# Merged row sums, a shorter last key tile and smaller weight pieces in an attention kernel that feeds a mixture of experts

## The chip, the cores and the metric

The kernel runs on one core of one Trainium2 chip. The metric is the device time of one launch in microseconds (us). A program on one core has no second core to compare with, so a run is called slow here when it is more than 1.5% above the fastest run of the same kernel in the same job, and fast otherwise.

## The reference, cut to what matters

```python
# attention: 4 batches, 8 heads, 768 positions, head size 64, fp32
keep  = is_global(first 8 keys) | is_local(0 <= i - j < 96)
scores = q @ k.T / 8 + bias(head, distance);  scores[~keep] = -1e9
a = exp(scores - max);  a = a / (sum(a) + 1e-9);  x = a @ v
# experts: 3072 tokens, 512 wide, 8 experts of 384 tokens each
logits = x @ w_gate                       # balanced greedy assignment of tokens to experts
out[mask] = relu(x[mask] @ w1[e]) @ w2[e]
```

The kernel works in three stages: attention over 16 head pairs (two heads of one batch at a time), routing (six rounds of a search on the vector engine), and the eight experts.

## The kernel before

Per head pair the tensor engine (PE) computes scores, the scalar engine (ACT) takes the exponential, the vector engine (DVE) multiplies a bias-and-mask table, and PE multiplies by v. Another engine, Pool, issues the weight loads. Then one function forms the row sums of the exponentials and the gate logits in the same two tiles `pr` in PSUM. Row halves (`rg`) and query quarters (`gq`) give eight combinations of 64 operand rows and 32 output rows; the page lists their matmuls as `64*32`, and the prediction calls a combination a tile. In the records of the phase at 118.82 us the first matmuls of the eight start 6 or 7 ns apart, while two of 151 columns in the same combination start 128 or 129 ns apart. `t` is the head of the pair. Cuts are marked with `# ...`.

```python
def scores(n, g):
    ps = ps_s.tile([128, 2, 512], FP32, tag="ps")
    for i, q0, o, w in PIECES[g]:            # three key tiles of 159 columns, and 24 of the last
        for c in range(2):                   # upper and lower half of the key tile
            qa = q0 + (56 * c if i < NT - 1 else 0)
            for t in range(2):
                # ... r: the 64 rows of head t
                nc.tensor.matmul(ps[64*c : 64*c + 64, t, o : o + w], lhsT=kA[r, i, 64*c : 64*c + 64],
                                 rhs=qTt[r, qa : qa + w], start=True, stop=True, ...)

def sums(n):
    pr = [ps_t.tile([128, 192], FP32, tag="pt", ...) for rg in range(2)]
    # for every (gq, rg): a list of (columns, onesx[.., t, :], Ps[n, g][.., t, columns]) over pieces and heads t
    # ... the lists are issued in turn, one matmul of each (gq, rg) after the other
    for gq in (0, 1, 2, 3):
        for rg in range(2):                  # gate logits of head rg
            nc.tensor.matmul(pr[rg][32*gq : 32*gq + 32, :], lhsT=wgx[64*rg : 64*rg + 64, j, :],
                             rhs=oTs[n][64*rg : 64*rg + 64, :, gq, :], start=False, stop=True, ...)

def sums_out(n, pr):                         # sums and logits to the token layout
    for rg in range(2):
        nc.vector.transpose(out=LT[:, rg], in_=pr[rg])
    nc.vector.tensor_tensor(out=rs[n], in0=LT[:, 0, :, 16:18], in1=LT[:, 1, :, 16:18], op=ALU.add)
    nc.vector.reciprocal(rs[n], rs[n])
    # ... gate logits times rs; x scaled by rs in tok_out; every fourth pair a reduction into L_sb

# the loop over head pairs, every engine in the order written:
for n in range(NP + 2):
    # scores and exp of pair n, first half; v product of pair n-1; x transposes of pair n-2;
    # k and q transposes of pair n+1; second halves
    weight_piece()                           # one 512 KB load of expert weights on the Pool queue
    # ... mask(n, 1); sums(n-1); sums_out(n-1, pr)
while wpieces:
    weight_piece()                           # the rest of them
```

The softmax here doesn't subtract the row's maximum and nothing guards it: scores larger than these inputs give would overflow.

## Time and profile before

| | kernel before |
|---|---|
| time, median of the first 3 runs | 366.54 us (361.71 to 382.19) |
| profiled run (375.11 us): span | 373.3 us |
| its attention, to the last matmul of the sums | 201.8 us |
| from there to the first expert matmul | 72.0 us |
| from there to the end | 99.5 us |
| records of PE up to the end of attention (8116 matmuls and weight loads, 79 others, nearly all semaphore instructions) | 8195 |
| 16,384-byte packets of PE's instruction queue | 39 |
| stops at borders of 256 instructions, summed | 38.5 us |
| half-clock time of PE inside attention | 29.7 us |

The last two are worked out from the records of the trace: all records of PE are put in order of start and numbered from 0; the stop at a border is the time from record k-1 to record k for k = 449 + 256j. The half-clock time sums the windows in which the granted clock was 0.5. The profiled run is a launch of its own and 3.7% slower than the fastest of the runs: by the rule above it is slow. The prediction below shows the lines of the page and of the waits.

### The profile page before, as it was taken

To read this page: it belongs to the slowest core of one execution; us is meant where nothing else is said; L and a number is where in the kernel's file an instruction comes from. 1 tells how busy PE (TensorE), PEld (TensorE's weight loads), DVE (VectorE), ACT (ScalarE), POOL (GpSimd) and SP (SyncE) were. 2 spreads that over 40 slices of the span, in tenths; PEclk is the share of its full clock that TensorE was granted. 3 is DMA by queue.
4 is the path that set the end of the run, shared out by engine and by line. 5 is a ranking of instruction groups with operands and counts; after the bars stand their busy time and mean duration, and the time that the engine had idled before them with its cause. 6 is when DMAs were issued, how large, how long until landed. Compare 5 with 4: busy or idle time off the path is not lost. (4 is left out here: it accounts for less than half of the span.)

```text
span 373.3 us, 10787 instructions
## 1 busy us (share of the span) xinstructions
PE 270.2 (72%) x4684; PEld 201.5 (54%) x4684; DVE 168.5 (45%) x421; ACT 104.4 (28%) x192; POOL 114.9 (31%) x170
## 2 busy tenths in 40 slices
PE   3678889885979679789777232222479999999990
PEld 2676778775958569677656111111245555555540
DVE  4154546641746436466353766678313322223310
ACT  1665324341524314343110000000023244432230
POOL 8342123330333303323603000000477545433221
PEclk9999999996989979899896555555569999999996
DMA  8997986985597983847999993000134323322111
GB/s 164 236 252 155 188 175 136 241 193 100 125 191 153 199 174 98 149 90 149 183 211 209 226 214 62 0 0 1 42 101 129 98 84 115 112 84 86 56 60 63
DMA packets 58376, 49.49 MB, mean 133 GB/s; under 512 B 32977, under 2 KB 51921, under 8 KB 58321
## 3 DMA queue, kind: packets, MB, share of 16 engines
q0 software_dynamic: 15808, 26.22, 34.6%
q1 hardware_dynamic: 42512, 22.50, 24.5%
q8 instruction: 39, 0.64, 0.7%
q14 instruction: 17, 0.13, 0.1%
HBM read 56.05 MB, written 9.44 MB: 175 GB/s over the span
## 5 line engine op out<-in xcount | busy, mean ns | idle before, releaser
L292 PE MATMUL ps<-qT,kA 64*64 64x159 f32 (+1 forms) x1024 | 43.7, 293 | 23.3 <-issue 18.6
L327 PE MATMUL po<-P,v 64*64 64x151 f32 (+8 forms) x1088 | 49.5, 283 | 14.0 <-issue 13.2
L292 PEld LDWEIGHTS ps<-qT,kA 64*64 64x64 f32 x1024 | 36.7, 141 | 34.7 <-issue 28.9
L300 ACT ACTIVATE P<-ps 128x1002 f32<-128x1002 f32 x32 | 32.3, 1008 | 75.9 <-PE ps L292 75.9
L327 PEld LDWEIGHTS po<-P,v 64*64 64x64 f32 x1088 | 43.0, 145 | 17.1 <-issue 16.0
L271 POOL COPY kA<-kA 128x56 f32<-128x56 f32 x16 | 16.5, 1030 | 116.2 <-DVE kA L267 99.4
L801 ACT ACTIVATE hT<-ph 128x384 bf16<-128x384 f32 x64 | 31.4, 490 | 71.7 <-PE ph L798 71.1
L781 POOL DMA_INDIRECT xe<-x_tok,idi x24 | 23.0, 959 | 80.1 <-DVE idi L638 62.9
L798 PE MATMUL ph<-xT,w_all 128*128 128x384 bf16 x256 | 44.9, 336 | 0.1
L306 DVE TENSOR_TENSOR P<-P,Wm 128x1002 f32<-128x1002 f32 x32 | 40.3, 1261 | 2.4 <-ACT P L300 2.4
L396 DVE TENSOR_TENSOR x<-pk,rs 128x384 bf16<-128x384 f32 x32 | 17.6, 557 | 44.7 <-PE pk L389 43.6
L798 PEld LDWEIGHTS <-w_all 128*128 128x128 bf16 x256 | 25.7, 100 | 18.8 <-issue 2.5
L811 POOL DMA_INDIRECT out_dram<-ot,idi x24 | 23.5, 981 | 35.9 <-DVE ot L810 32.7
L355 PE MATMUL pr<-P,onesx 64*32 64x24 f32 (+18 forms) x1408 | 32.8, 263 | 0.0
L355 PEld LDWEIGHTS pr<-P,onesx 64*32 64x32 f32 x1408 | 29.5, 116 | 2.2
L810 DVE COPY ot<-po 128x512 f32<-128x512 f32 x24 | 16.6, 692 | 29.2 <-PE po L807 29.2
L788 DVE COPY xT<-pxe 128x512 bf16<-128x512 bf16 x24 | 9.5, 422 | 44.0 <-PE pxe L787 43.2
L807 PEld LDWEIGHTS <-hT 128*128 128x128 bf16 x192 | 18.2, 98 | 19.5
L807 PE MATMUL po<-w_late,hT 128*128 128x512 bf16 x96 | 21.9, 379 | 0.0
L807 PE MATMUL po<-w_early,hT 128*128 128x512 bf16 x96 | 21.9, 379 | 0.0
L258 PE MATMUL pt<-ident,kn 128*128 128x128 f32 x96 | 17.4, 302 | 5.2 <-POOL Dm L132 5.2
L336 DVE COPY oT<-po 128x384 f32<-128x384 f32 x16 | 8.9, 558 | 22.7 <-PE po L327 22.7
(146 smaller groups left out, 315.7 us busy)
## 6 DMA issues: line engine op xcount, KB each, us to landing
w_all<-in_moe_w_dram POOLq DMA_DIRECT2D x16, 512.0 KB, 10.0
v<-in_v_dram SPq DMA_DIRECT2D x32, 180.0 KB
kr<-in_k_dram SPq DMA_DIRECT2D x15, 384.0 KB
qr<-in_q_dram SPq DMA_DIRECT2D x15, 384.0 KB
w_early<-in_moe_w_dram POOLq DMA_DIRECT2D x8, 512.0 KB, 8.8
w_late<-in_moe_w_dram POOLq DMA_DIRECT2D x4, 1024.0 KB, 20.0
x_tok<-x SPq DMA_DIRECT2D x16, 192.0 KB
v<-in_v_dram SPq DMA_DIRECT2D x32, 14.0 KB
```

The source lines that it names most:

```text
L258: nc.tensor.transpose(pt[:, jj, :], kn[:, 3 * hf + jj, :, :].rearrange("p t d -> p (t d)"), ident)
L292: nc.tensor.matmul(ps[64 * c : 64 * c + 64, t, o : o + w], lhsT=kA[r, i, 64 * c : 64 * c + 64], rhs=qTt[r, qa : qa + w], start=True, stop= ...
L300: nc.scalar.activation(P, ps[:, :, 0:GW], AF.Exp, scale=0.125)
L306: nc.vector.tensor_tensor(out=P, in0=P, in1=Wm[:, h0 : h0 + 2, QW * g : QW * g + GW], op=ALU.mult)
L327: mm = nc.tensor.matmul(po[n][bk][64 * t : 64 * t + 64, a - QB * bk : z - QB * bk], lhsT=v7[r, t, i, :], rhs=Ps[n, g][r, t, off : off + z ...
L355: nc.tensor.matmul(pr[rg][32 * gq : 32 * gq + 32, a:z], lhsT=l_, rhs=r_, start=first[gq, rg], stop=True, skip_group_check=True)
L396: between[0] = nc.vector.tensor_tensor(out=xs[b][:, 3 * hf : 3 * hf + 3, 128 * j : 128 * j + 128].rearrange("p c (h d) -> p c h d", d=D_), ...
L781: nc.gpsimd.indirect_dma_start(out=xe, out_offset=None, in_=x_tok[:, :], in_offset=bass.IndirectOffsetOnAxis(ap=idi[:, s : s + 1], axis=0),)
L798: nc.tensor.matmul(ph, lhsT=w1_all[:, e, kc, 128 * fc : 128 * fc + 128], rhs=xT_e[:, kc, :, :].rearrange("p t n -> p (t n)"), start=(kc == ...
L801: nc.scalar.activation(hT[:, fc, :], ph, AF.Relu)
L807: nc.tensor.matmul(po, lhsT=hT[:, fc, 128 * t : 128 * t + 128], rhs=w2_of(e)[:, fc, :], start=(fc == 0), stop=(fc == NFC - 1))
L811: s = nc.gpsimd.indirect_dma_start(out=out[:, :], out_offset=bass.IndirectOffsetOnAxis(ap=idi[:, TSLAB * e + t : TSLAB * e + t + 1], axis= ...
```

## The change

Its intent: half as many matmuls and weight loads for the row sums, because both heads of a pair lie side by side in one matmul; no score matmuls for the half of the last key tile that holds no keys; and weight loads in smaller pieces among the pairs. The core of the diff (the bias table only moves to another buffer, and `ps` becomes one fixed tile whose unused part is zeroed once):

```diff
-                for c in range(2):
-                    qa = q0 + (56 * c if i < NT - 1 else 0)
+                for c in range(2 if i < NT - 1 else 1):
...
-            pr = [ps_t.tile([128, 192], FP32, tag="pt", ...) for rg in range(2)]
+            pr = [ps_t.tile([128, 2, 192], FP32, tag="pt", ...) for rg in range(2)]
...
-                        for t in range(2):
-                            l.append((..., onesx[64 * rg : 64 * rg + 64, t, :],
-                                      Ps[n, g][64 * rg : 64 * rg + 64, t, off : off + z - a]))
+                    lists[gq, rg] = [(..., onesx, Ps[n, g][64 * rg : 64 * rg + 64, :, off : off + z - a])
+                                     for g, i, off, a, z in windows(rg, 192 * gq, 192 * gq + 192)]
+            lists[0, 1].append((0, 56, zerox, Ps[n, 0][64:128, :, 0:56]))
...
-            for rg in range(2):
-                nc.vector.transpose(out=LT[:, rg, :, :].rearrange("p b c -> p (b c)"), in_=pr[rg])
-            nc.vector.tensor_tensor(out=rs[n], in0=LT[:, 0, :, 16:18], in1=LT[:, 1, :, 16:18], op=ALU.add)
-            nc.vector.reciprocal(rs[n], rs[n])
+            nc.scalar.copy(out=LS, in_=pr[0])
+            nc.vector.tensor_tensor(out=LS, in0=LS, in1=pr[1], op=ALU.add)
+            nc.vector.transpose(out=LT.rearrange("p t b c -> p (t b c)"), in_=LS.rearrange("p t q -> p (t q)"))
+            nc.vector.reciprocal(rs[n], LT[:, :, :, 16].rearrange("p t b -> p b t"))
...
-            for hf in range(2):
-                wpieces.append((w1_all[:, e, 2 * hf : 2 * hf + 2, :], ...))      # 512 KB
+            for kc in range(NKC):
+                wpieces.append((w1_all[:, e, kc, :], ...))                         # 256 KB
...
                 weight_piece()
+                if n % 2:
+                    weight_piece()
```

More of the change, by code (lines that the diff above doesn't have):

```diff
@@ L126 @@
     Wm = consts.tile([128, H_, NW], FP32)
-    Dm = consts.tile([128, NW], FP32)
-    FAR = 1.0e5
-    for hf in range(2):
-        blk = Dm[64 * hf : 64 * hf + 64, QW : 2 * QW]
-        base = N_GLOBAL * (1 - hf)
-        nc.gpsimd.iota(blk, pattern=[[1, QW]], base=base, channel_multiplier=-1,
-                       allow_small_or_imprecise_dtypes=True)
-        nc.gpsimd.affine_select(out=blk, in_=blk, compare_op=ALU.is_ge, fill=FAR,
-                                base=base, pattern=[[1, QW]], channel_multiplier=-1)
-        nc.gpsimd.affine_select(out=blk, in_=blk, compare_op=ALU.is_ge, fill=FAR,
-                                base=N_LOCAL - 1 - base, pattern=[[-1, QW]], channel_multiplier=1)
-    nc.gpsimd.tensor_copy(out=Dm[:, 0:QW], in_=Dm[:, QW : 2 * QW])
-    G0 = Dm[0:N_GLOBAL, :]
-    for o_ in (0, QW):
-        nc.gpsimd.memset(G0[:, o_ : o_ + QW], FAR)
-        nc.gpsimd.memset(G0[:, o_ : o_ + KT], float(N_LOCAL))
-    nc.gpsimd.affine_select(out=G0[:, 0:60], in_=G0[:, 0:60], compare_op=ALU.is_ge, fill=FAR,
-                            base=-1, pattern=[[-1, 60]], channel_multiplier=1)
-    nc.gpsimd.affine_select(out=G0[:, 60:KT], in_=G0[:, 60:KT], compare_op=ALU.is_ge, fill=FAR,
-                            base=60 - N_LOCAL, pattern=[[1, 60]], channel_multiplier=-1)
-    for m_ in (2, 3):
-        nc.gpsimd.tensor_copy(out=Dm[:, m_ * QW : m_ * QW + QW], in_=Dm[:, QW : 2 * QW])
-    nc.gpsimd.tensor_copy(out=Dm[:, 4 * QW : NW], in_=Dm[:, QW + 24 : QW + 48])
     wg_sb = consts.tile([128, NKC, N_EXP], FP32)
@@ L153 @@
     nc.gpsimd.memset(wgx, 0.0)
-    onesx = consts.tile([128, 2, 32], FP32)
+    onesx = consts.tile([128, 32], FP32)
     nc.gpsimd.memset(onesx, 0.0)
-    for t in range(2):
-        nc.gpsimd.memset(onesx[:, t, 16 + t : 17 + t], 1.0)
+    nc.gpsimd.memset(onesx[:, 16:17], 1.0)
+    zerox = consts.tile([128, 32], FP32)
+    nc.gpsimd.memset(zerox, 0.0)
     L_sb = lpool.tile([128, NCHUNK, N_EXP], FP32)
@@ L197 @@
         ps_t = actx.enter_context(tc.tile_pool(name="ps_t", bufs=4, space=bass.MemoryType.PSUM))
+        Dm = xp.tile([128, NW], FP32, tag="x")
+        FAR = 1.0e5
+        for hf in range(2):
+            blk = Dm[64 * hf : 64 * hf + 64, QW : 2 * QW]
+            base = N_GLOBAL * (1 - hf)
+            nc.gpsimd.iota(blk, pattern=[[1, QW]], base=base, channel_multiplier=-1,
+                           allow_small_or_imprecise_dtypes=True)
+            nc.gpsimd.affine_select(out=blk, in_=blk, compare_op=ALU.is_ge, fill=FAR,
+                                    base=base, pattern=[[1, QW]], channel_multiplier=-1)
+            nc.gpsimd.affine_select(out=blk, in_=blk, compare_op=ALU.is_ge, fill=FAR,
+                                    base=N_LOCAL - 1 - base, pattern=[[-1, QW]], channel_multiplier=1)
+        nc.gpsimd.tensor_copy(out=Dm[:, 0:QW], in_=Dm[:, QW : 2 * QW])
+        G0 = Dm[0:N_GLOBAL, :]
+        for o_ in (0, QW):
+            nc.gpsimd.memset(G0[:, o_ : o_ + QW], FAR)
+            nc.gpsimd.memset(G0[:, o_ : o_ + KT], float(N_LOCAL))
+        nc.gpsimd.affine_select(out=G0[:, 0:60], in_=G0[:, 0:60], compare_op=ALU.is_ge, fill=FAR,
+                                base=-1, pattern=[[-1, 60]], channel_multiplier=1)
+        nc.gpsimd.affine_select(out=G0[:, 60:KT], in_=G0[:, 60:KT], compare_op=ALU.is_ge, fill=FAR,
+                                base=60 - N_LOCAL, pattern=[[1, 60]], channel_multiplier=-1)
+        for m_ in (2, 3):
+            nc.gpsimd.tensor_copy(out=Dm[:, m_ * QW : m_ * QW + QW], in_=Dm[:, QW : 2 * QW])
+        nc.gpsimd.tensor_copy(out=Dm[:, 4 * QW : NW], in_=Dm[:, QW + 24 : QW + 48])
         NB = 3
@@ L238 @@
         for e in range(N_EXP):
-            for hf in range(2):
-                wpieces.append((w1_all[:, e, 2 * hf : 2 * hf + 2, :],
-                                moe_w1[e].rearrange("(kc p) f -> p kc f", p=128)[:, 2 * hf : 2 * hf + 2, :]))
+            for kc in range(NKC):
+                wpieces.append((w1_all[:, e, kc, :], moe_w1[e, 128 * kc : 128 * kc + 128, :]))
             if e < W2_EARLY:
-                for hf in range(2):
-                    wpieces.append((w2_early[:, e, 4 * hf : 4 * hf + 4, :],
-                                    moe_w2[e].rearrange("(fc p) d -> p fc d", p=128)[:, 4 * hf : 4 * hf + 4, :]))
+                for hf in range(4):
+                    wpieces.append((w2_early[:, e, 2 * hf : 2 * hf + 2, :],
+                                    moe_w2[e].rearrange("(fc p) d -> p fc d", p=128)[:, 2 * hf : 2 * hf + 2, :]))
         def weight_piece():
@@ L282, in qT_out @@
                 in_=pt.rearrange("c j p -> c p j"))
+        ps = ps_s.tile([128, 2, 512], FP32)
         def scores(n, g):
             kA, qTt = kAs[n % 2], qTs[n % 2]
-            ps = ps_s.tile([128, 2, 512], FP32, tag="ps")
             for i, q0, o, w in PIECES[g]:
-                for c in range(2):
-                    qa = q0 + (56 * c if i < NT - 1 else 0)
+                for c in range(2 if i < NT - 1 else 1):
                     for t in range(2):
@@ L292, in scores, with expo @@
                         nc.tensor.matmul(ps[64 * c : 64 * c + 64, t, o : o + w], lhsT=kA[r, i, 64 * c : 64 * c + 64],
-                                         rhs=qTt[r, qa : qa + w], start=True, stop=True, skip_group_check=True)
-            return ps
+                                         rhs=qTt[r, q0 + 56 * c : q0 + 56 * c + w], start=True, stop=True,
+                                         skip_group_check=True)
         Ps = {}
-        def expo(n, g, ps):
+        def expo(n, g):
             P = pp.tile([128, 2, GW], FP32, tag="P")
@@ L340, in sums @@
             j = n % NPAIR
-            pr = [ps_t.tile([128, 192], FP32, tag="pt", name=f"pr{n}_{rg}") for rg in range(2)]
+            pr = [ps_t.tile([128, 2, 192], FP32, tag="pt", name=f"pr{n}_{rg}") for rg in range(2)]
             lists = {}
@@ L344, in sums @@
                 for rg in range(2):
-                    l = lists[gq, rg] = []
-                    for g, i, off, a, z in windows(rg, 192 * gq, 192 * gq + 192):
-                        for t in range(2):
-                            l.append((a - 192 * gq, z - 192 * gq, onesx[64 * rg : 64 * rg + 64, t, :],
-                                      Ps[n, g][64 * rg : 64 * rg + 64, t, off : off + z - a]))
+                    lists[gq, rg] = [(a - 192 * gq, z - 192 * gq, onesx, Ps[n, g][64 * rg : 64 * rg + 64, :, off : off + z - a])
+                                     for g, i, off, a, z in windows(rg, 192 * gq, 192 * gq + 192)]
+            lists[0, 1].append((0, 56, zerox, Ps[n, 0][64:128, :, 0:56]))
             first = dict.fromkeys(lists, True)
@@ L353, in sums @@
                     if l:
-                        a, z, l_, r_ = l.pop(0)
-                        nc.tensor.matmul(pr[rg][32 * gq : 32 * gq + 32, a:z], lhsT=l_, rhs=r_,
-                                         start=first[gq, rg], stop=True, skip_group_check=True)
+                        a, z, w_, r_ = l.pop(0)
+                        nc.tensor.matmul(pr[rg][32 * gq : 32 * gq + 32, :, a:z], lhsT=w_[64 * rg : 64 * rg + 64, :],
+                                         rhs=r_, start=first[gq, rg], stop=True, skip_group_check=True)
                         first[gq, rg] = False
-            for gq in (0, 1, 2, 3):
+            for gq in range(4):
                 for rg in range(2):
-                    nc.tensor.matmul(pr[rg][32 * gq : 32 * gq + 32, :], lhsT=wgx[64 * rg : 64 * rg + 64, j, :],
+                    nc.tensor.matmul(pr[rg][32 * gq : 32 * gq + 32, rg, :], lhsT=wgx[64 * rg : 64 * rg + 64, j, :],
                                      rhs=oTs[n][64 * rg : 64 * rg + 64, :, gq, :], start=False, stop=True,
@@ L371, in sums_out @@
             LT = sp.tile([128, 2, NBLK, 32], FP32, tag="LT", bufs=1)
-            for rg in range(2):
-                nc.vector.transpose(out=LT[:, rg, :, :].rearrange("p b c -> p (b c)"), in_=pr[rg])
+            LS = sp.tile([128, 2, 192], FP32, tag="LS", bufs=1)
+            nc.scalar.copy(out=LS, in_=pr[0])
+            nc.vector.tensor_tensor(out=LS, in0=LS, in1=pr[1], op=ALU.add)
+            nc.vector.transpose(out=LT.rearrange("p t b c -> p (t b c)"), in_=LS.rearrange("p t q -> p (t q)"))
             rs[n] = sp.tile([128, NBLK, 2], FP32, tag="rs", name=f"rs{n}", bufs=3)
-            nc.vector.tensor_tensor(out=rs[n], in0=LT[:, 0, :, 16:18], in1=LT[:, 1, :, 16:18], op=ALU.add)
-            nc.vector.reciprocal(rs[n], rs[n])
+            nc.vector.reciprocal(rs[n], LT[:, :, :, 16].rearrange("p t b -> p b t"))
             if j == 0:
@@ L411 @@
                 nc.vector.memset(v7s[i][:, :, NT - 1, :], 0.0)
+            nc.vector.memset(ps[64:128, :, 3 * QW : GW], 0.0)
             load_qk(0)
@@ L433 @@
                 if n < NP:
-                    ps = scores(n, 0)
-                    expo(n, 0, ps)
+                    scores(n, 0)
+                    expo(n, 0)
                 if n + 1 < NPAIR:
@@ L463 @@
                     mask(n, 0)
-                    ps = scores(n, 1)
-                    expo(n, 1, ps)
+                    scores(n, 1)
+                    expo(n, 1)
                 if 1 <= n <= NP:
```

## The prediction

> **What bounds the kernel now.** I read the page's slices first, to find the stages; then a table of three stretches; then, in the long one, what the tensor engine waited for; then its order of time around a few of those waits.
>
> ```profile
> PE   3678889885979679789777232222479999999990
> PEclk9999999996989979899896555555569999999996
> DMA  8997986985597983847999993000134323322111
> ```
>
> Each digit is a slice of 9.3 us. PE is busy but not full up to slice 21 (attention), nearly idle at half clock in slices 22 to 28 (routing), full from 30 (experts). DMA is high in the first stage and for a little of the second.
>
> ```profile
> core 0: us, PE busy (x) PEld busy (x) DVE busy (x) ACT busy (x) POOL busy (x), PEclk, DMA share, GB/s
> 12.00:202.00 190.00, 155.71 (x4046) 136.83 (x4046) 93.54 (x187) 67.32 (x115) 58.64 (x75) 0.92 0.81 170
> 202.00:265.00 63.00, 19.43 (x90) 11.99 (x82) 44.91 (x158) 1.90 (x7) 0.90 (x2) 0.53 0.48 85
> 265.00:373.00 108.00, 92.06 (x544) 50.37 (x544) 26.15 (x48) 31.37 (x64) 46.55 (x48) 0.91 0.26 89
> ```
>
> The change touches only the first row, so it is worth what it takes out of those 190 us. There PE is the busiest engine (156 of 190), DVE has half its time free and ACT two thirds. The waits of PE in that stretch:
>
> ```profile
> PE ps L292 <- issue: 18.6, 12, 4.2
> PE po L327 <- issue: 13.2, 11, 2.4
> PE ps L292 <- POOL kn L235: 3.5, 1, 3.5
> PE ps L292 <- ACT P L300: 1.2, 1, 1.2
> ```
>
> 31.8 us of idle PE are put down to "issue", a wait for nothing that the profile sees, and hardly anything to another engine. Two of them in order of time:
>
> ```profile
> 127.49 0.75 PE L327 MATMUL po<-P,v 64*64 64x7 f32 x19
> 130.17 0.86 PE L327 MATMUL po<-P,v 64*64 64x127 f32 x17 [1.93 <-issue]
> ...
> 134.39 0.53 PE L292 MATMUL ps<-qT,kA 64*64 64x159 f32 x7
> 137.14 0.89 PE L292 MATMUL ps<-qT,kA 64*64 64x159 f32 x23 [2.22 <-issue]
> ```
>
> PE stops in the middle of a run of equal instructions. Counting matmul and weight-load records in order of start, the stops fall at number 449, 705, 961, 1217 and so on: always 256 further. And
>
> ```profile
> q8 instruction: 39, 0.64, 0.7%
> ```
>
> is 39 packets of 16,384 bytes[...]. I take PE's own instruction stream as what it waits for. In the packet records, the packet for a block starts 0.2 to 5.3 us (mean 3.0) after PE began the block before it, takes 0.9 to 1.7 us, and where PE was waiting it goes on about 1.4 us after the packet has landed. Measured from start to start across these borders, the 31 blocks from number 449 to 8129 cost 38.5 us, 1.24 us each. The wait is long behind weight traffic: where the queue of the weight loads filled over 0.4 of the DMA engines before the packet, it began 3.1 to 5.3 us after the block; where it did not, mostly 0.2 to 2.4. So **the attention stage is PE-bound with an instruction supply that falls behind**. A stretch without a stop, 144.0 to 152.3, holds 263 matmuls at full clock with PE busy throughout: about 8.0 us for the 254 matmuls of one head pair, against a mean period of 11.5 us over pairs 1 to 15. Stops come to 1.98 blocks x 1.24 = 2.5 us of the difference; the rest is mainly the clock: seven half-clock windows, 30 us in all, lie between 83 and 202 us, around the longer stops.
>
> [...]
>
> **The change part by part.**
>
> *Row sums.* The sums matmul, one of the page's groups:
>
> ```profile
> L355 PE MATMUL pr<-P,onesx 64*32 64x24 f32 (+18 forms) x1408 | 32.8, 263 | 0.0
> ```
>
> 1408 / 16 pairs = 88 records a pair, where the program has 44 matmuls: an fp32 matmul leaves two records, each with its weight load. The new program has 22 merged ones and one that writes zeros: 46 records. So 42 matmuls and 42 weight loads less per pair. The columns streamed do not shrink (two heads side by side, plus 112 zero columns), and the starts show the array rather than issue as limit: two passes of 151 columns in one tile start 129 ns apart, 96 columns 83 ns, about 0.86 ns a column. The longest tile has 732 columns, two passes: 1.26 us against 1.5 measured for the phase at full clock (118.88 to 120.39). I credit 0.1 us a pair for less unevenness.
>
> *Empty half of the last tile.* 4 program matmuls less per pair, 8 records of 24 columns. The other half still streams: 0.05 us.
>
> *PE stream in all.* Per pair 254 matmuls become 254 - 42 - 8 = 204, with weight loads 508 instructions become 408: 1.98 blocks become 1.59, over 16 pairs 31.75 become 25.5.
>
> *New evacuation.* Before: two transposes of 192 columns (362 ns each), an add (172), reciprocal (228), multiply (257) = 1.38 us on DVE. After: an ACT copy of 384 columns from PSUM (like L280, 572 ns), a DVE add of 384 columns with one PSUM operand (like L396, 557), one transpose of 384 (estimate 650), reciprocal, multiply: 0.57 us more on ACT, 0.3 more on DVE, and 0.9 us later to the row scales. The scales are needed when PE has done scores, attend and three transposes, about 2.3 us after the sums; the new chain takes 2.27. It just fits; I charge 0.1 us a pair.
>
> *Weight pieces.* In the loop the 18 calls issued 18 x 512 KB = 9.4 MB; now 27 x 256 KB = 7.1 MB, one piece after even pairs, two after odd. Total weight traffic is unchanged: 21 pieces instead of 6 are left for the end, 5.5 MB against 3.1. At the some 215 GB/s of slices 20 to 22 the 2.4 MB more take 11 us, inside a routing stage whose DMA is idle from slice 24 on. Hidden, then; the gain is a shorter queue in front of the instruction fetch in pairs 0 to 13. The last two pairs stay saturated either way.
>
> *Placement of the bias table.* Some Pool memsets come before it; half a microsecond of start-up at most, counted as zero.
>
> **The sum.** PE work per pair stays 8.0 us (-0.15, +0.1), but a block now lasts 8.0 / 1.59 = 5.0 us in place of 4.0. A fetch that came a given time after the block's start is hidden for 1.0 us longer: subtracting 1.0 from each of the 31 measured stops leaves 17 us, 0.56 each, and 25.5 of them cost 14 us. Gain 24 us. Half-clock windows cost, at most half of 30 us x 0.8 PE share = 12 us; shorter stops should save some 4. Shorter weight queues: with weights the fetch lags 2 us more than without, and a quarter less traffic should save some 0.2 us on each of 25 fetches, 4 us. Against it, pairs that run faster put the same q, k, v bytes into less time, DMA share 0.81 to about 0.9: 4 us back. Net 28 us, 366.5 - 28 = **338 us**.
>
> **Rivals.**
> (a) *The fetch is not hidden but paced*: if DMA gets busier as pairs get shorter, each fetch begins later and every block stops as long as before. Then only 6.25 blocks x 1.24 = 8 us go: 358. For it: a DMA share of 0.81 already. Against it: bytes per pair fall from about 1.7 to 1.6 MB, and blocks without weight traffic show hardly a stop.
> (b) *PE's compute is the limit and instructions are free*: then the change is worth 1 or 2 us and the new evacuation may eat it: 365. The stops at every 256th instruction speak against it.
> (c) *The new DVE and ACT chain becomes the wait*: up to 0.9 us x 16 = 14 us given back, 352. DVE at half load and ACT at a third speak against a rate limit; the chain's length is the risk.
> (d) *Weights late for the experts*: experts begin some 60 us after attention, the rest (5.5 + 4.2 MB, some 45 us) starts before attention ends; unlikely.
> (e) *Better than counted*: nearly all stops vanish, and the cold clock with them: 16 x 8.1 us and the start, 320.
>
> **Range and chances.** Mixing (a) and (c) on one side and (e) on the other, with runs of the kernel before spread from 361.7 to 382.2: 325 to 353 us. Faster by over 2% (below 359) 0.94, within 2% 0.05, slower 0.01.
>
> **What would show it.** Right: about 33 instruction packets instead of 39, "issue" waits of PE in attention at 10 to 18 us, pair periods about 9.7, sums phase still about 1.4 us at full clock, routing and experts unchanged at 63 and 108. Wrong: stops per block still at 1.2 us (a); PE waiting for DVE or ACT at the x transposes (c); PE waiting for weights in the experts (d).

24 us for stops, 4 for the clock and 4 for shorter weight queues, less 4 for a busier DMA, came to the 28 us of the forecast. That a packet goes with 256 instructions is in the trace: before each of the 31 borders in attention, and after the border before it, exactly one packet starts (24 borders and 24 packets in the changed kernel). "At most half" for the half clock is too: the experts' matmuls of 384 columns (L798, kernel before) start 320 ns apart at half clock and 163 at full. The 650 ns of the long transpose was the estimate, below twice the 362 ns of the short one; it took 578. The 4 us for the clock was an estimate too, about a third of the 12, and no run shows that share.

## More of the kernel before

One more line, of the page's transfers (name, queue, count, size, median us from issue to landing), is needed later:

```profile
w_all<-in_moe_w_dram POOLq DMA_DIRECT2D x16, 512.0 KB, 10.0
```

## The result, and the profile after

The changed kernel took 339.02 us in the median of 4 runs (337.47 to 340.65), beside 369.77 us for the kernel before (4 runs, 361.71 to 382.19). The ratio of the fast runs is 0.931, with a 95% interval of 0.918 to 0.944. Here and below a ratio is the mean time of one kernel's fast runs over that of the other's fast runs of the same rounds, so it is not quite the ratio of the medians. The profiled run of the changed kernel (339.29 us) is a fast run, that of the kernel before (375.11 us) is not, so differences between the two profiles (35.8 us of span) are larger than that of the fast means (364.1 and 339.0 us, 25 us apart).

The slices of the changed kernel's page, one digit per 8.4 us:

```profile
PE   2589898899999879987622222253999999999960
PEclk9999999999999999998655555555799999999995
DMA  7988869986999775899999990002342224112220
```

Attention now ends in slice 19 instead of 21 (the first is slice 0), and PE's clock stays full up to slice 17, where before it dipped in six slices from 9 to 21. The three stages, by the same ends as in the table above:

```profile
12.00:164.00 152.00, 136.39 (x3246) 118.60 (x3246) 99.73 (x172) 74.73 (x130) 63.96 (x89) 0.98 0.88 192
164.00:235.60 71.60, 22.01 (x102) 13.63 (x100) 46.51 (x160) 2.38 (x8) 12.45 (x17) 0.52 0.66 123
235.60:337.50 101.90, 90.19 (x530) 49.02 (x528) 24.85 (x45) 31.44 (x64) 41.11 (x43) 0.94 0.25 88
```

The first two columns are the stretch and its length; then busy time and count of PE, PE weight loads, DVE, ACT and Pool; then granted clock, DMA share and GB/s. Attention ends 37.8 us earlier (164.0 against 201.8), routing takes the same (71.6 against 72.0), and the last stage is 2.4 us longer. In attention PE is busy for 136 us, 19 less, and the stretch became 38 us shorter: half of the gain is idle time of PE (34 us to 16), the other half busy time, which grows when the clock is halved (the sums and gates of a pair took 3.0 us at half clock and 1.8 at full in the kernel before). The waits of PE in that stretch:

```profile
PE po L327 <- issue: 5.6, 4, 1.8
PE ps L292 <- POOL kn L236: 3.6, 1, 3.6
PE ps L292 <- issue: 3.2, 4, 1.1
PE pr L353 <- issue: 1.7, 2, 1.2
PE ps L292 <- ACT P L300: 1.2, 1, 1.2
PE pt L276 <- DVE x L395: 1.1, 3, 0.4
```

"issue" fell from 31.8 us to 11.6 (5.6 + 3.2 + 1.7 + 1.1, the last from a line not shown), and no other engine took its place (PE's waits for the x scaling on DVE come to 1.9 us, 1.1 of them in the last line shown). The instruction queue and the sums:

```profile
q8 instruction: 32, 0.52, 0.7%
...
L353 PE MATMUL pr<-P,onesx 64*32 64x286 f32 (+12 forms) x704 | 27.2, 321 | 1.7 <-issue 1.7
...
w_all<-in_moe_w_dram POOLq DMA_DIRECT2D x32, 256.0 KB, 9.0
```

There are 32 instruction packets instead of 39. The sums are 704 records with ones where there were 1408, and each streams twice the columns. A piece of `w_all`, of half the size, still takes 9.0 us to land where the whole one took 10.0; the DMA share of this stretch is 0.88. The stops that remain lie at the same kind of place:

```profile
107.79 0.50 PE L292 MATMUL ps<-qT,kA 64*64 64x159 f32 x8
109.08 0.78 PE L292 MATMUL ps<-qT,kA 64*64 64x159 f32 x18 [0.79 <-issue]
```

This is record 4289 = 449 + 15 x 256, in the middle of the scores. All the stops in attention, and what else the records give:

| | before | after |
|---|---|---|
| blocks of 256 instructions in attention after record 449 | 31 | 24 |
| stops at their borders, sum (mean of one) | 38.5 us (1.24) | 15.6 us (0.65) |
| packet start after the start of the block before, mean | 3.01 us | 2.98 us |
| mean period of pairs 1 to 15 (shortest) | 11.5 us (9.9) | 9.1 us (8.0) |
| first to last start of a pair's sums and gates, without a stop | 1.80 us | 1.58 us |
| half-clock time in attention | 29.7 us | 5.3 us |

The changed kernel was profiled a second time in run 12 below (339.42 us): stops 11.8 us, mean delay of the packet 2.65 us, half-clock time 17.1 us, 6.8 of them at the start. So the stops of the two differ by 4 us, while the half-clock time of one profile says little about the next.

### The profile page after: what moved, and what is told of

Its sections match the earlier page's. It is cut to its first block, busy times and chain, and to the rows that moved or that the text cites. A ratio compares the mean times of both kernels' runs of the same rounds, so it can differ in the third digit from the quotient of the medians.

```text
span 337.5 us, 9192 instructions
## 1 busy us (share of the span) xinstructions
PE 251.6 (75%) x3884; PEld 183.5 (54%) x3884; DVE 175.0 (52%) x406; ACT 112.2 (33%) x208; POOL 126.3 (37%) x194
## 5 line engine op out<-in xcount | busy, mean ns | idle before, releaser
L327 PE MATMUL po<-P,v 64*64 64x151 f32 (+8 forms) x1088 | 42.0, 268 | 6.5 <-issue 5.6
L292 PE MATMUL ps<-qT,kA 64*64 64x159 f32 (+1 forms) x896 | 38.5, 298 | 8.0 <-POOL kn L236 3.6
L306 DVE TENSOR_TENSOR P<-P,Wm 128x1002 f32<-128x1002 f32 x32 | 42.3, 1323 | 2.3 <-ACT P L300 2.3
L292 PEld LDWEIGHTS ps<-qT,kA 64*64 64x64 f32 x896 | 33.4, 137 | 16.8 <-issue 11.0
L327 PEld LDWEIGHTS po<-P,v 64*64 64x64 f32 x1088 | 37.3, 136 | 8.0 <-issue 6.9
L300 ACT ACTIVATE P<-ps 128x1002 f32<-128x1002 f32 x32 | 32.3, 1009 | 22.9 <-PE ps L292 22.9
L813 POOL DMA_INDIRECT out_dram<-ot,idi x24 | 23.6, 982 | 36.1 <-DVE ot L812 31.7
L353 PE MATMUL pr<-P,onesx 64*32 64x286 f32 (+12 forms) x704 | 27.2, 321 | 1.7 <-issue 1.7
L250 POOL DMA_DIRECT2D w_all<-in_moe_w_dram x32 | 17.4, 548 | 11.5 <-DMA w_all<-in_moe_w_dram 8.9
L353 PEld LDWEIGHTS pr<-P,onesx 64*32 64x32 f32 x704 | 17.8, 108 | 7.0 <-issue 3.2
L258 PE MATMUL pt<-ident,kn 128*128 128x128 f32 x96 | 16.7, 293 | 5.6 <-POOL onesx L132 5.6
```

The lines of the kernel that those rows point to most:

```text
L250: nc.gpsimd.dma_start(dst, s_)
L292: nc.tensor.matmul(ps[64 * c : 64 * c + 64, t, o : o + w], lhsT=kA[r, i, 64 * c : 64 * c + 64], rhs=qTt[r, q0 + 56 * c : q0 + 56 * c + w], ...
L300: nc.scalar.activation(P, ps[:, :, 0:GW], AF.Exp, scale=0.125)
L306: nc.vector.tensor_tensor(out=P, in0=P, in1=Wm[:, h0 : h0 + 2, QW * g : QW * g + GW], op=ALU.mult)
L327: mm = nc.tensor.matmul(po[n][bk][64 * t : 64 * t + 64, a - QB * bk : z - QB * bk], lhsT=v7[r, t, i, :], rhs=Ps[n, g][r, t, off : off + z ...
L353: nc.tensor.matmul(pr[rg][32 * gq : 32 * gq + 32, :, a:z], lhsT=w_[64 * rg : 64 * rg + 64, :], rhs=r_, start=first[gq, rg], stop=True, ski ...
```

## The experiments

Theory S: the supply of PE's instructions sets the pace of attention; fewer instructions for the same array work make a block of 256 last longer, so the next block arrives in time more often. Rivals: C or T, PE's array work and its clock set the pace and the number of instructions doesn't matter; W, the smaller weight pieces did it; Q, the packets are late because of the q, k and v loads. Each part was first done alone, and instructions were put back. Runs 1 to 4 are one job and share its runs of the kernel before (fast mean 367.9 us, worked out as a fast mean over its ratio; three of eleven runs are fast, and one took 1345 us). Runs 5 to 8 and 9 to 12 are two more jobs, each on another chip.

**1. The merged sums alone.** The changed kernel with the old weight pieces and the old two halves of the last tile.

```diff
# against the changed kernel
-                for c in range(2 if i < NT - 1 else 1):
+                for c in range(2):
...
-            for kc in range(NKC): wpieces.append(...256 KB...)
+            for hf in range(2): wpieces.append(...512 KB...)
-                if n % 2:
-                    weight_piece()
```

> The merged row sums and their new evacuation alone; weights and the last key tile as in the kernel before. PE instructions per pair 508 - 84 = 424. Theory S (PE's instruction supply sets the pace of attention): 26.5 blocks instead of 31.75, each lasting about 0.8 us longer, stops at block borders fall from 38.5 us to about 18 to 24, time 345 to 353 us. Rival C (PE's array work sets the pace, instructions are free): the streamed columns are the same, so 364 to 370 us. Rival W (the weight pieces are what helped): 364 to 370 us.

Measured: 345.27 us in the median (339.63 to 346.33), ratio 0.928 (0.892 to 0.964). Its profiled run is a slow one: stops of 24.1 us, 33 instruction packets. The median is at the lower end of S's range, the mean of its two fast runs (341.5 us) below it; C and W, which expected no change, are out. Nearly all of the gain is in this part.

**2. The last tile's empty half alone.**

```diff
# against the kernel before
-                for c in range(2):
+                for c in range(2 if i < NT - 1 else 1):
```

> The last key tile without its empty half alone. PE instructions per pair 508 - 16 = 492, 30.75 blocks. Theory S: each block lasts 0.13 us longer and there is one block less, so stops fall by 4 to 6 us: 360 to 365 us if the kernel before runs at 367. Rival C: 0.05 us a pair, 366 us. The two are near each other; the stops in the trace tell more than the time.

Measured: 365.4 us (360.8 to 369.18), ratio 0.986 (0.966 to 1.006): unclear. Stops 33.6 us in a slow profile. The direction is S's and the size too, but the interval includes 1.

**3. The 256 KB pieces alone.**

```diff
# against the kernel before
-            for hf in range(2): wpieces.append(...512 KB...)
+            for kc in range(NKC): wpieces.append(...256 KB...)
+                if n % 2:
+                    weight_piece()
```

> The 256 KB weight pieces alone, all else as in the kernel before. The 31.75 blocks stay. Theory S with the weight queue as what delays the fetch: mean delay of an instruction packet after the start of the block before falls from 3.0 to about 2.5 us, stops from 38.5 to 25 to 32 us, time 355 to 362 us. Rival (the delay does not come from weights but from the q, k, v loads): stops stay at 36 to 40 us, 366 us.

Measured: 366.55 us (362.4 to 368.8), ratio 0.993 (0.976 to 1.010). In its profile, a slow run, packets started 2.78 us after the block before and stops were 35.8 us. My expectation of 355 to 362 us missed; smaller pieces with a quarter less traffic are worth little by themselves.

**4. Instructions put back.** The changed kernel with 50 matmuls of 4 columns per pair into unused columns of the tiles of the sums (the result is not touched).

```diff
# against the changed kernel, at the end of sums(n); prf is a tile of 512 columns, pr its first 384
+            for m_ in range(50):
+                gq, rg = (m_ // 2) % 4, m_ % 2
+                nc.tensor.matmul(prf[rg][32*gq : 32*gq + 32, 384:388], lhsT=ones_bf[64*rg : 64*rg + 64, 0:32],
+                                 rhs=ones_bf[64*rg : 64*rg + 64, 0:4], start=False, stop=True, ...)
```

> The changed kernel with 50 tiny matmuls (4 columns, bf16, into unused columns of the sums bank) per pair at the end of the sums: 100 PE instructions more, so again 508 a pair, with next to no array work. Theory S: blocks are again 31.75 and short; stops at block borders rise from 15.6 us to 25 to 35 us and the time to 352 to 364 us, more than the tiny matmuls' own time (estimate 0.4 to 0.8 us a pair, 6 to 12 us). Rival C: stops stay near 15 us and only the own time is added, 345 to 351 us.

Measured: 371.37 us (366.64 to 374.68), ratio to the kernel before 1.002 (0.982 to 1.023). With 508 instructions a pair again, **the whole gain is gone**. The tiny matmuls add 0.51 us from first to last start of a pair's sums (2.09 against 1.58 without a stop), 8.2 us in all; the mean of the fast runs rose by 29.6 (from 339.0 to 368.6, in two jobs). In its profile, a slow run, attention ends at 198.7 us and stops are 36.1 us. PE's longest waits in its attention:

```profile
PE ps L292 <- issue: 22.3, 11, 4.6
PE pr L354 <- issue: 4.5, 5, 1.4
PE ps L292 <- POOL kn L236: 3.8, 1, 3.8
PE pk L394 <- issue: 3.3, 1, 3.3
```

"issue" is back at 30 us, and nothing else has come. The time exceeded the upper end of what I expected, presumably because I had left the clock out: 29.6 us of attention ran at half clock again.

**5. The control: tensor time without instructions.** Three fp32 matmuls of 128 columns at the same place, 12 instructions instead of 100.

```diff
# against the changed kernel, same place
+            for m_ in range(3):
+                nc.tensor.matmul(prf[0][0:32, 384:512], lhsT=onesx[0:64, :], rhs=ident[0:64, :],
+                                 start=False, stop=True, ...)
```

> Control for the tiny matmuls: the changed kernel with 3 fp32 matmuls of 128 columns, all in one tile, at the same place. They should take the same tensor time as the 50 tiny ones did (those took about 0.65 us from first to last start; 6 records of about 0.11 us) but are 12 instructions a pair instead of 100. Theory S (instruction supply): stops stay near 15 us, time = 339 + the own 10 us or a little less, 345 to 350 us. Rival T (the tiny matmuls cost so much because PE has 10 us more work and goes through it at a cold clock): 365 us or more, as with the tiny ones.

Measured: 338.15 us (337.65 to 343.21), as much as without them, where the lowest of the expectations was 345. The sums phase is 0.33 us longer (1.91 against 1.58), 5.3 us in all, somewhat less than the 8.2 of the tiny ones; stops are 10.4 us (fast run). PE's "issue" waits in attention are 6.6 us in all, 0.4 of them in a line not shown:

```profile
PE pr L354 <- issue: 1.9, 2, 1.0
PE pk L392 <- issue: 1.7, 1, 1.7
PE pr L359 <- issue: 1.6, 2, 1.2
PE pt L276 <- issue: 1.0, 1, 1.0
```

So this added array work cost nothing that shows, and the added instructions of run 4 cost far more than their own time. T, which expected 365 us or more, is out.

**6 and 7. No weights among the pairs.** The changed kernel and the kernel before, with all early weight pieces issued after the loop.

```diff
# against the changed kernel (6), and likewise against the kernel before (7)
-                weight_piece()
-                if n % 2:
-                    weight_piece()
```

> The changed kernel without any expert weights among the head pairs: all 48 pieces are issued after the loop's last instruction on the Pool queue. Theory W (weights in front of the instruction packet make it late): mean delay from 3.0 to about 2 us, stops before the end of the attention from 15.6 to 3 to 8 us, attention ends 8 to 14 us earlier. In all 325 to 335 us if the weights, which now have some 80 us of transfer left at the end, still come before the experts want them; else 340 or more with PE waiting for gathers or weights. Rival Q (q, k, v loads delay the packet): stops stay at 13 to 17 us.

> The same with the kernel before: its 24 pieces all after the loop. Theory W: mean delay from 3.0 to about 2 us; stops from 38.5 to 12 to 20 us, attention ends 20 to 30 us earlier, time 340 to 350 us. Rival Q: stops stay at 33 to 40 us and the time at 365 to 372 us.

Measured for the changed kernel: **326.81 us** (325.85 to 328.49). Packets start 1.26 us after the block before, stops are 2.2 us in all, and attention ends at 147.2 us, 17 us earlier, which is more than I expected. (The weights now begin to move at 131.8 us, over the last two pairs.) PE's longest waits there:

```profile
PE ps L292 <- POOL kn L236: 3.7, 1, 3.7
PE po L327 <- issue: 1.5, 1, 1.5
PE ps L292 <- ACT P L300: 1.2, 1, 1.2
```

Pairs now take 8.0 us each (every fourth 8.6). Measured for the kernel before: 347.13 us (340.54 to 351.34); its profiled run, the fast one, has stops of 12.2 us and packets at 1.90 us (the 38.5 and 3.01 of the kernel before are of a slow run, so part of that difference may be the state). Q would have left the stops where they were. So weight traffic among the pairs makes most of the stops, and of the packet's delay of 3.0 us it makes 1.7 in the changed kernel and 1.1 in the kernel before. The two remedies, longer blocks and earlier packets, each work alone. Only one of the seven runs of the kernel before in this job counts as fast, so no ratio is given; by the fastest run of each kernel of the job it is 361.3 us before, 340.5 without weights among the pairs, 337.7 with the shorter program (run 5) and 325.9 with both: gains of 21, 24 and 35 us. They overlap, since a stop can be removed only once. What is given back stands at the other end: PE waited 9.0 us for the first gathered rows where the changed kernel waits 4.3. The packets of the trace show why: weight packets fill their queue until 217 us, and the first gather, issued on the same queue at 211.1 us, has its first packets at 216; in the changed kernel the weights are through by 204 us and the first gather is issued at 228.5.

**8. The evacuation doubled.**

```diff
# against the changed kernel
             nc.scalar.copy(out=LS, in_=pr[0])
+            nc.scalar.copy(out=LS, in_=pr[0])
+            nc.vector.tensor_tensor(out=LT..., in0=LS, in1=pr[1], op=ALU.add)
             nc.vector.tensor_tensor(out=LS, in0=LS, in1=pr[1], op=ALU.add)
```

> The changed kernel with the ACT copy and the DVE add of the sums' evacuation done twice: 0.5 us more on ACT, 0.56 us more on DVE and 1.0 us more between the sums and the row scales of each pair. If this chain lies off the path that sets the pace, as the waits of the changed kernel suggest (PE waited 1.9 us in all for the x scaling): 0 to 3 us more, 339 to 342 us. If it is on the path: up to 16 x 1.0, 350 to 355 us.

Measured: 345.77 us (341.42 to 348.12); the fast runs average 343.2, 4 us over the changed kernel. Neither expectation holds: the shortest pairs are 8.8 instead of 8.0 us, and in its profile (a slow run) a wait has grown from 1.1 us to 9.5:

```profile
PE pt L276 <- DVE x L397: 9.5, 12, 1.5
```

The q transposes wait for the x scaling to free their PSUM buffer. So the chain from the sums to the scales has next to no slack left: of 1.0 us added, 0.8 shows in a pair without stops. Over the whole kernel less shows, presumably where a stop comes anyway.

**9 and 12. The weight pieces on top of the rest.** The changed kernel with the old pieces, and the changed kernel itself once more, in the same rounds.

> The changed kernel with the weight pieces of the kernel before (512 KB, one after each pair): what the new pieces are worth on top of the shorter instruction stream. From the sums alone (345.3 us) and all three parts (339.0 us): 342 to 345 us if the pieces carry half or more of the difference, 339 to 341 us if the empty half carries it. Stops at block borders 17 to 22 us against 15.6.

> The changed kernel once more, on the same chip and in the same rounds as the run with the old weight pieces, to compare the two directly: 337 to 342 us.

Measured: 341.86 us (340.0 to 351.9) with the old pieces, ratio 0.915 (0.907 to 0.922) to a kernel before that ran at 378.53 us in the median in this job; 338.95 us (337.14 to 343.26) for the changed kernel, ratio 0.909 (0.900 to 0.918). The fast means differ by 2.4 us (341.2 and 338.8) and the intervals overlap: at most a small gain, not shown apart from nothing. The stops of run 9, in a slow profile, are 22.6 us, of run 12, in a fast one, 11.8.

**10 and 11. Two attempts to improve on 6.** The second matrices of the last two experts written behind the first gathers (10), and besides, the gate reduction of every fourth pair moved behind the next mask (11).

```diff
# 10, against run 6
-    for e in range(W2_EARLY, N_EXP): nc.gpsimd.dma_start(w2_late[...], moe_w2[e]...)
+    for e in range(W2_EARLY, N_EXP - 2): load_w2(e)
...                                             # in experts(), after load_x(e + 1), once
+                while w2_behind: load_w2(w2_behind.pop(0))
# 11, besides
-                nc.vector.tensor_reduce(out=L_sb[...], in_=Gb[b]..., op=ALU.add)     # in sums_out
+                gates.append(b)                                   # done after mask(n + 1, 0)
```

> The changed kernel with all early weights after the loop (326.8 us) and, besides, the second matrices of the last two experts (2 MB) issued behind the first gathers instead of in front of them. There PE waited 9.0 us for the first gather where the changed kernel waits 4.3. If that is the weights still in the queue ahead of the gathers, 2 MB at some 215 GB/s is 9 us and the wait goes back to about 4.3: 321 to 324 us. If not, 326 to 328 us.

> As the run with the last weights behind the gathers, and the gate reduction (0.86 us on DVE, every fourth pair) moved from the evacuation chain to a place behind the next mask. Without stops every fourth pair took 8.6 us where the others took 8.0. If the DVE chain between the sums and the x scaling is on the path, those three pairs fall to 8.0 and the time by 1.5 to 2 us against that run; if not, no difference.

Measured for 10: 325.56 us (324.86 to 329.41). The experiment did not test what it was meant to: in the built program the four loads of those matrices still stand together ahead of the gathers, presumably because outside the loop over pairs the order of instructions is not the one written. PE waited 7.8 us for the first gather, so it is a repeat of run 6 within the spread, and whether moving those loads would shorten the wait stays open. Measured for 11: **323.85 us** (323.52 to 324.57), ratio to the kernel before 0.869 (0.863 to 0.875). The three pairs of 8.6 us became 8.0 and the fast mean fell by 2.2 us: the reduction was on the path. Its attention, from the end of pair 0:

```profile
26.50:145.00 118.50, 116.88 (x2987) 103.84 (x2983) 93.93 (x164) 64.78 (x113) 43.85 (x54) 1.00 0.71 167
```

PE is busy 116.9 of 118.5 us at full clock. This version is correct and beats both kernels. It is also steady: 6 runs lie within 1.1 us, where the kernel before spreads over 12.6 us in the same job.

## Why the prediction was right

- **What bounds attention.** The prediction took it as PE-bound with an instruction supply that falls behind. Runs 4 and 5 show it: 100 instructions put back cost the whole gain, array work without instructions nothing. Rivals (a), that each fetch stops as long as before, and (b), that instructions are free, fall: a stop averages 0.65 us instead of 1.24. The prediction says that it counts matmul and weight-load records; its numbers 449, 705 and so on come out only when the semaphore instructions are counted with them, as in the table above.
- **The stops.** Predicted 14 us left, measured 15.6 (11.8 in run 12). Of the reasoning (same delay of the packet, block 1.0 us longer) the first half shows directly: the mean delay is 2.98 us against 3.01.
- **Row sums.** Credited 0.1 us a pair for a smoother phase; it is 0.22 (1.80 to 1.58), 3.5 us in all. Whether the 42 weight loads less per pair have a part in it, no run shows.
- **The clock.** This term was probably too small. I gave 4 us to fewer half-clock windows; they fell from 29.7 us to 5.3 in one profile of the changed kernel and to 17.1 in the other. At half clock the experts' matmuls of 384 columns started 320 ns apart instead of 163, and the sums and gates of a pair took 3.0 us instead of 1.8. If half of the half-clock time is lost, an estimate from the first of these, the term is worth up to 12 us by the one profile and up to 6 by the other. With 22.9 us of stops and 3.5 of sums the 12 add up to 38, what attention gained between the two profiles, but the part of the clock was not measured apart.
- **Weight pieces.** Credited 4 us for shorter queues and charged 4 for a busier DMA. The DMA share rose from 0.81 to 0.88, as expected, and the delay of the packet did not move. The last two pairs stayed saturated, as expected: a DMA share of 1.13 from 178 us on in the kernel before, of 1.15 from 144 us on in the changed one. Whether two effects cancelled, as in the sum, or neither was there, is not shown. By themselves the pieces show no gain clear of noise (run 3).
- **Evacuation.** "It just fits" was right for most pairs: the new chain takes 2.1 us where 2.27 were reckoned (ACT copy 479 ns, transpose 578), and run 8 shows that the slack is used up. In every fourth pair, with the gate reduction on top, it did not fit (8.6 us instead of 8.0, run 11). Rival (c) did not come true, but by little.
- **Routing and experts.** Predicted unchanged. Routing is. After the last scatter of the experts the changed kernel needs 9.7 us to the end, the kernel before 7.8. All nine profiles with 48 weight pieces have 9.6 to 10.1 there, all five with 24 pieces 7.7 to 8.0. It goes with the number of weight pieces; why was not tested.

That the time came out at 339.0 against 338 is in part luck. Pairs gained more than predicted (9.1 against 9.7 us), and the end gave 2 us back. And the 28 us of gain were worked out from the profile of a run of 375.1 us but taken off the median of 366.5: between the two profiled runs the gain was 35.8 us, between the fast means 25. What is not luck is the mechanism and, as far as two profiles show, the size of the stops.

## What to carry to other kernels

When PE idles in the middle of a run of equal matmuls and the profile names no releaser, count the instructions between the stops. If the count is always the same, as the 256 here, suspect that PE waits for its program; here an instruction saved was then worth more than the array time it took (run 4: 1600 instructions with 8.2 us of work of their own cost 29.6 us). Remedies are fewer and wider matmuls (339.0 us instead of 364.1, with the other two parts), and keeping large loads out of a dense stretch when a later stage leaves the DMA idle (run 6: 326.8 us instead of 339.0, by the medians). Before trusting either, put cheap instructions back and put array work back: the pair of runs tells the causes apart.

## What else the records show of PE's instructions and its clock

- The 31 borders in attention cost 38.5 us of 190 in the profiled run of the kernel before (15.6 for 24 borders in the changed kernel), and 100 instructions a pair more (run 4) brought the fast mean from 339.0 to 368.6 us, for 8.2 us of work of their own.
- In attention of the kernel before a block's packet starts 0.2 to 5.3 us after PE began the block before it, never earlier, and where PE stopped it goes on some 1.4 us after the packet landed (in the changed kernel 0.5 to 4.9 us, and some 1.4 as well).
- The mean delay of a packet was 3.0 us with weights among the pairs and 1.3 (changed kernel) or 1.9 (kernel before) without.
- The half-clock stretches of attention last 3.41 us, or 6.83. In the kernel before there are seven, and they begin during or within 2 us after its seven longest stops; six of these lasted only 2.2 to 2.6 us, the seventh 4.45. In the changed kernel the one stretch begins 2.2 us after a stop of 1.96 us, while a stop of 2.03 us elsewhere has none. In run 11, whose stops sum to 1.4 us, there is no such stretch; run 10, whose longest stop is 1.2 us, has one of 3.41 us all the same. What sets a stretch off is therefore not shown.
